# Token DFT in a spectral mixer: the fifth channel block accumulates T1, and a group has 28 steps in place of 32

## The chip, the cores and the metric

The kernel runs on one core of a Trainium2 chip, as one program. The core has a matrix engine (PE, which writes its results into eight banks called PSUM), a vector engine (DVE), a scalar engine (ACT), GpSimd (POOL) and SyncE (SP); the last two mostly issue DMA transfers here. Every engine takes its instructions in the order of the program and waits for semaphores of the others. The metric is the time of one execution in microseconds, the median of several runs.

## What is computed

The input `x` has 2048 tokens of 640 channels. The output is the sum of `x`, a two-dimensional Fourier transform of the normalized input (real part), and an MLP over the tokens:

```python
xn = _layernorm(x)
a = einsum("bsd,ed->bse", xn, dft_hid_re);  b = einsum("bsd,ed->bse", xn, dft_hid_im)
y = einsum("ts,bse->bte", dft_seq_re, a) - einsum("ts,bse->bte", dft_seq_im, b)
...
u = gelu(einsum("bsd,sf->bdf", _layernorm(xn), w1) + b1)
out = x + y + transpose(einsum("bdf,fs->bds", u, w2) + b2)
```

All values are float32.

## The kernel before

**Stages.** The kernel does the transform over tokens first (the "column" stage), stores its real and imaginary halves in DRAM (`y_part`), then does the transform over channels (`hidden`), then the two halves of the MLP (`up`, `down`). Only the column stage is touched.

**Float32 by three matmuls.** A float32 operand is cut in two: `high` copies it into a rounded format (ACT), and `low` subtracts the rounded copy from the original (DVE). `three` then multiplies high by high, high by low and low by high, all into one bank. Of the two operands of a column product, the channels of `x` stand in SBUF already cut (`fixed`), and the matrix is cut piece by piece: `cut_piece` makes a piece of 128 by 512 with one `high` (line 138) and one `low` (line 141). Three buffers take the pieces in turn.

**A group.** `columns` makes one group of the column stage: 512 output tokens `c`, for one half `h` of the input tokens. There are seven groups (a first block of columns is made by `first_columns`); the first three of them have `h` = 0 and store with plain writes, the last four have `h` = 1 and add to what stands in DRAM (`store_y`, lines 455 and 457, both from POOL's queue). In a group, four matrix blocks B11, B21 (real) and B12, B22 (imaginary), each of four pieces q = 0 to 3, meet five blocks of 128 channels. The first four channel blocks are done as a two by two block product with seven products in place of eight (Winograd's form of Strassen's scheme), for which the blocks of the matrix are replaced in place by T1 = B12 - B11, T3 = B22 - B12, T2 = B22 - T1 and T4 = B21 - T2. Products 1, 2, 5, 6, 3, 7 and 4 take B11, B21, T1, T2, B22, T3 and T4. Each takes six matmuls for a piece: three for each of two halves e = 0, 1 of 128 channels.

**The fifth channel block** takes part in no such scheme: it needs the plain sums F0 = A1 B11 + A2 B21 and F1 = A1 B12 + A2 B22, where A1 and A2 are its upper and lower rows of tokens. Its three matmuls ride on the pieces of product 1 (B11), 2 (B21) and 3 (B22). No product of the scheme takes B12 plain, so B12 is cut as a piece of its own ("product 8"), with no other matmuls than those three. A group thus has 32 pieces or steps, with 9, 3 or 6 matmuls each, 216 in all.

**What sets the order.** A hand-written turn (`turn_of`) emits for step i, on every engine: the loads due, the reads of banks, the `high` of step i + 2, the differences of matrix blocks (`extras`), a few jobs that prepare later stages (`do_jobs`, at the turns listed in `JOBS_AT`, in turns modulo `GROUP`), the `low` of step i + 2, and then the matmuls of step i. All offsets in `columns` count turns from the group's first step.

**Reading the banks.** Sums leave a bank in two ways: `fresh` copies a bank to one of the `c` tiles on ACT (line 601), and `more` adds a bank to the `c` tile on DVE (line 612) and stores it. There are six `c` tiles, which are handed out in turn by `c_tile`; a tile that comes round again is written only after the store that last read it has landed. C11, C12, C22 and C21 each have two halves e; F0 and F1 have one bank each (`psum[4]` and `psum[7]`). In the last group (`g == 2 * NC - 2`) C22 and C12 are not summed on DVE: each of their two parts is copied and stored by itself.

Of the kernel before, what the change touches and what calls it, by code (L numbers as in the profile page):

```python
# [17 lines left out]
F = 1728  # L18
# [8 lines left out]
NC = S // CH  # L27
# [23 lines left out]
    M6 A6 H4 T6 N4 B6 L4 b11 P5 H5 M7 A7 R6-7 T7 N5 B7 F6-7 L5 b12 e1 P6  # L51
    H6 T8 M8 A8 N6 B8 L6 b13 P7 H7 T9 M12 A12 N7 B9 L7
"""
GROUP = 32

JOBS_AT = (
    ((0, 1, 2, 3, 4, 5, 10, 20, 21, 26, 27, 30, 31), (0, 1, 2, 3, 20), ()),
    ((0, 1, 2, 3, 20, 21, 27, 31), (), (9, 11, 25)),  # L60
)


# [6 lines left out]
def fnet_plus_mixer(  # L70
# [30 lines left out]
    nc = tc.nc  # L101
# [41 lines left out]
    def sub(to, a, b):  # L143
        nc.vector.tensor_sub(to, a, b)  # L144

    def three(psum, w, m, first, last):

        (wh, wl), (mh, ml) = w, m
        nc.tensor.matmul(psum, wh, mh, start=first, stop=False, skip_group_check=True)  # L149
        nc.tensor.matmul(psum, wh, ml, start=False, stop=last and wl is None, skip_group_check=True)  # L150
        if wl is not None:
            nc.tensor.matmul(psum, wl, mh, start=False, stop=last, skip_group_check=True)  # L152
# [17 lines left out]
    def cut_piece(source, n, tail=False, stacked=False):  # L170

        held = {}

        def of_tail():
            hi, src = (t.rearrange("p (q c) -> p q c", c=P) for t in (held["piece"][:, 0, :n], source()))
            return hi[:, :, :TAIL], hi[:, :, P - TAIL :], src[:, :, :TAIL]

        def top():  # L180
            cut_turn[0] = (cut_turn[0] + 1) % (AHEAD + 1)
            held["piece"] = keep.tile([P, 2, D], R32, name="piece", tag=f"cut{cut_turn[0]}")
            if tail:
                hi, _, src = of_tail()
                high(hi, src)
            else:
                high(held["piece"][:, 0, :n], source())

        def bottom():
            if tail:  # L190
                hi, lo, src = of_tail()
                low(lo, src, hi)
                return held["piece"][:, 0, :n], None
            hi, lo = (held["piece"][:, i, :n] for i in range(2))
            if stacked:
                last = slice(n - P, n)
                low(hi[TAIL:, last], source()[TAIL:, last], hi[TAIL:, last])
            whole = n - P if stacked else n
            low(lo[:, :whole], source()[:, :whole], hi[:, :whole])
            return hi, lo  # L200

        return top, bottom
# [89 lines left out]
    def fifth(a, which, i):  # L292
        return a[:, which, 7 * Q + i * P : 7 * Q + (i + 1) * P]
# [154 lines left out]
    def c_tile():  # L448

        i = c_turn[0] = (c_turn[0] + 1) % 6  # L450
        return c_place[i // 3][:, i % 3, :]

    def store_y(h, m, c, j, t):
        if h == 0:
            nc.gpsimd.dma_start(y_part[m][c][:, j, :], t)
        else:
            nc.gpsimd.dma_start(y_part[m][c][:, j, :], t, accum_op=ALU.add)
# [76 lines left out]
    def columns(g, h, c):  # L534

        s0 = len(steps)
        raw = [pieces[(g + m) % 2] for m in range(2)]
        banks, cs = {}, {}

        def load(name, q):  # L540
            i, m = int(name[1]) - 1, int(name[2]) - 1
            nc.sync.dma_start(raw[m][:, i, q, :], dft_seq[m * NC + c, 8 * h + q + 4 * i])

        for name, at in (("B11", (-6, -5, -5, -4)), ("B21", (-3, -3, -2, -2)), ("B12", (-2, -1, 0, 0)), ("B22", (1, 2, 3, 4))):
            for q in range(4):
                loads[s0 + at[q]].append(lambda name=name, q=q: load(name, q))

        def b(name, q, n=1):
            t = raw[int(name[2]) - 1][:, int(name[1]) - 1]
            return t[:, q, :] if n == 1 else t[:, q : q + n, :]  # L550

        order = [(1, q) for q in range(4)] + [(i, q) for q in range(4) for i in (2, 8)]
        order += [(i, q) for i in (5, 6) for q in range(4)]
        order += [(3, 0), (3, 1)] + [(7, q) for q in range(4)] + [(3, 2), (3, 3)] + [(4, q) for q in range(4)]
        operand = {1: "B11", 2: "B21", 5: "B11", 6: "B11", 3: "B22", 7: "B12", 8: "B12", 4: "B21"}
        for names, at in (
            (("B11", "B12", "B11"), (6, 8)), (("B11", "B22", "B11"), (13, 15)), (("B12", "B22", "B12"), (17, 18)),
            (("B21", "B21", "B11"), (22, 24)),  # L560
        ):
            for e in range(2):
                extras[s0 + at[e]].append(lambda names=names, e=e: sub(*(b(n, 2 * e, 2) for n in names)))

        bank_of = {1: "z", 6: "z", 7: "z", 4: "z", 5: "y", 3: "y", 2: "w"}
        bank_at = {"z": 2 - 2 * (g % 2), "y": 2 * (g % 2), "w": 5}
        fifth_of = {1: (0, 0), 2: (0, 1), 8: (1, 0), 3: (1, 1)}

        def products(i, q):
            def run(w):
                a = fixed[h][q]
                if q == 0 and i in (1, 2, 5):
                    for e in range(2):
                        banks[bank_of[i], e] = psum[bank_at[bank_of[i]] + e]
                if i in fifth_of:
                    m, low_rows = fifth_of[i]
                    first = q == 0 and i in (1, 8)
                    if first:  # L580
                        banks["f", m] = psum[4 + 3 * m]
                    three(
                        banks["f", m], (fifth(a, 0, low_rows), fifth(a, 1, low_rows)), w,
                        first, q == 3 and i in (2, 3),
                    )
                if i in bank_of:
                    for e in range(2):
                        at = slot[i] * Q + e * P
                        three(
                            banks[bank_of[i], e], (a[:, 0, at : at + P], a[:, 1, at : at + P]), w,  # L590
                            q == 0 and i in (1, 2, 5), q == 3,
                        )
            return run

        for i, q in order:
            steps.append(cut_piece(lambda i=i, q=q: b(operand[i], q), CH) + (products(i, q),))

        def fresh(name, at, key, e, then=None):
            def run():
                cs[name, e] = c_tile()  # L600
                nc.scalar.activation(cs[name, e], banks[key, e], AF.Copy)
                if then:
                    store_y(h, *then, cs[name, e])
            reads[s0 + at].append(run)

        def more(name, at, key, e, then):
            if g == 2 * NC - 2 and name != "C11":

                return fresh(name, at, key, e, then)

            def run():
                nc.vector.tensor_add(cs[name, e], banks[key, e], cs[name, e])
                store_y(h, *then, cs[name, e])
            reads[s0 + at].append(run)

        for e in range(2):
            fresh("C11", 4, "z", e)
            more("C11", 11 + e, "w", e, (0, c, e))
            last = g == 2 * NC - 2
            fresh("C22", 16, "y", e, (1, c, 2 + e) if last else None)  # L620
            fresh("C12", 20, "z", e, (1, c, e) if last else None)
            more("C12", 28 + e, "y", e, (1, c, e))
            more("C22", 26 + e, "z", e, (1, c, 2 + e))
            fresh("C21", 32, "z", e, (0, c, 2 + e))
        fresh("F0", 13, "f", 0, (0, c, 4))
        fresh("F1", 30, "f", 1, (1, c, 4))


    moving = {}
# [370 lines left out]
    for g in range(2 * NC - 1):  # L1000
        columns(g, (g + 1) // NC, (g + 1) % NC)
    s_rows = BLOCK
    s_half = BLOCK + (NC - 1) * GROUP
    s_hid = len(steps)
# [73 lines left out]
    with tc.manual_schedule():  # L1078
        for word in START.split():
            start[word[0]](*map(int, word[1:].split("-")))  # L1080
        for i in range(8, len(steps) + 1):
            n_jobs, short = (1, i < BLOCK), False
            if BLOCK <= i < s_hid - 6:
                *n_jobs, light = [(i - BLOCK) % GROUP in at for at in JOBS_AT[i >= s_half]]
                if light:
# [47 lines left out]
```

## Time and profile before

| | |
|---|---|
| median of 3 runs | 876.68 us (876.0 to 876.92) |
| the profiled execution, its own time | 875.92 us |
| its span (first to last instruction) | 874.2 us |
| PE busy | 869.0 us, 4924 matmuls |
| DVE busy | 711.7 us |
| ACT busy | 530.2 us |
| seven column groups, by PE | 61.97 to 405.36 us |

The profile is of one execution. Its page gives busy time by engine, the span in 40 slices, the chain of work that ended last, and groups of instructions by line of the kernel. A row of a group reads: line, engine, operation, output and input tiles with shapes, count, then busy time, mean of one in ns, and the idle time of that engine just before them with what ended it. A window row gives for each engine its busy time in the stretch and in brackets how many instructions were in it.

### The profile page before, as it was taken

The page shows a single profiled execution, that of the slowest core. Times are in us where ns is not written, and L with a number is a line of the kernel's source. Part 1 is how long each engine was busy: PE and PEld are TensorE (multiplying, and loading weights), DVE is VectorE, ACT ScalarE, POOL GpSimd, SP SyncE. Part 2 cuts the span into 40 slices and gives each one's busy share as a digit, 9 for nine tenths or more (in the row PEclk, how much of TensorE's full clock was granted, in tenths as well). Part 3 has the DMA queues.
Part 4 walks back from the last instruction along what each step waited for, and adds up shares of the span by engine and source line. Part 5 has one row for each costly group of instructions (what it writes and reads, how often), then busy time and mean ns, then how long its engine had stood idle before and what let it go on. Part 6 is the DMA issues. An engine that isn't in the chain of part 4 may idle for free.

```text
span 874.2 us, 13999 instructions
## 1 busy us (share of the span) xinstructions
PE 869.0 (99%) x4924; PEld 793.1 (91%) x4924; DVE 711.7 (81%) x1217; ACT 530.2 (61%) x960; POOL 126.2 (14%) x170
## 2 busy tenths in 40 slices
PE   9999999999999999999999999999999999999998
PEld 6888888888888888889999999999999999999998
DVE  7878878795887978788887787998678978897887
ACT  5746576764556566557565556675577766555553
POOL 0110100101121111222010101000212221111211
PEclk9999999999999999999999999999999999999999
DMA  7771554619385556869666756454678797766786
GB/s 270 231 266 76 194 203 132 242 59 357 54 219 92 163 119 133 208 92 195 168 127 166 156 139 196 162 177 138 142 170 181 169 244 193 190 136 133 151 173 139
DMA packets 86087, 147.64 MB, mean 169 GB/s; under 512 B 8512, under 2 KB 35904, under 8 KB 85760
## 3 DMA queue, kind: packets, MB, share of 16 engines
q1 hardware_dynamic: 64928, 95.80, 34.0%
q0 software_dynamic: 20800, 50.70, 30.6%
q8 instruction: 38, 0.62, 0.3%
q14 instruction: 33, 0.27, 0.1%
q10 hardware_dynamic: 288, 0.25, 0.1%
HBM read 99.96 MB, written 52.00 MB: 174 GB/s over the span
## 4 chain that ended last, share of the span: by engine, by line
PE 94%; DVE 3%; ACT 1%; DMA 1%; issue 1%; DVEq 0%; ACTq 0%
PE psum L149 30%; PE psum L150 30%; PE psum L152 29%; PE psum L477 5%; DVE piece L141 1%; DMA pieces<-y 1%; DVE pieces L144 0%; DMA x<-in_x 0%; ACT piece L138 0%; ACT n L259 0%; ACT x L259 0%; DVE pair L144 0%; DVE st L210 0%; DVE pieces L785 0%; DVE shid L141 0%
## 5 line engine op out<-in xcount | busy, mean ns | idle before, releaser
L141 DVE TENSOR_TENSOR piece<-pieces,piece 128x512 fp32r<-128x512 f32 (+2 forms) x524 | 350.1, 671 | 125.8 <-ACT piece L138 119.1
L138 ACT ACTIVATE piece<-pieces 128x512 fp32r<-128x512 f32 (+3 forms) x508 | 318.1, 627 | 212.0 <-PE psum L152 143.5
L150 PE MATMUL psum<-piece,n 128*128 128x512 f32 x504 | 196.4, 390 | 0.0
L149 PE MATMUL psum<-piece,n 128*128 128x512 f32 x504 | 196.2, 389 | 0.0
L152 PE MATMUL psum<-piece,n 128*128 128x512 f32 x504 | 196.1, 389 | 0.0
L149 PE MATMUL psum<-sup,piece 128*128 128x320 f32 x392 | 121.2, 310 | 0.0
L149 PE MATMUL psum<-sdown,piece 128*128 128x320 f32 x392 | 121.0, 309 | 0.0
L150 PE MATMUL psum<-sup,piece 128*128 128x320 f32 x392 | 120.9, 309 | 0.0
L150 PE MATMUL psum<-sdown,piece 128*128 128x320 f32 x392 | 120.9, 309 | 0.0
L152 PE MATMUL psum<-sup,piece 128*128 128x320 f32 x376 | 116.6, 310 | 0.0
L152 PE MATMUL psum<-sdown,piece 128*128 128x320 f32 x376 | 116.2, 309 | 0.0
L144 DVE TENSOR_TENSOR pieces<-pieces 128x512 f32<-128x512 f32 (+3 forms) x142 | 112.7, 794 | 2.6
L150 PEld LDWEIGHTS psum<-piece,n 128*128 128x128 f32 x504 | 94.6, 188 | 21.0 <-DVE piece L141 1.5
L149 PEld LDWEIGHTS psum<-piece,n 128*128 128x128 f32 x504 | 94.6, 188 | 19.9
L152 PEld LDWEIGHTS psum<-piece,n 128*128 128x128 f32 x504 | 94.6, 188 | 19.3
L152 PE MATMUL psum<-shid,piece 128*128 128x320 f32 x280 | 86.6, 309 | 0.1
L150 PE MATMUL psum<-shid,piece 128*128 128x320 f32 x280 | 86.5, 309 | 0.0
L149 PE MATMUL psum<-shid,piece 128*128 128x320 f32 x280 | 86.5, 309 | 0.0
L854 ACT ACTIVATE pair<-psum 128x320 f32<-128x320 f32 x102 | 44.5, 436 | 54.6 <-PE psum L152 49.8
L149 PEld LDWEIGHTS psum<-sup,piece 128*128 128x128 f32 x392 | 73.6, 188 | 0.6 <-ACT pairs L854 0.3
L149 PEld LDWEIGHTS psum<-sdown,piece 128*128 128x128 f32 x392 | 73.6, 188 | 0.2 <-ACT pair L852 0.2
L150 PEld LDWEIGHTS psum<-sup,piece 128*128 128x128 f32 x392 | 73.6, 188 | 0.0
(106 smaller groups left out, 1115.8 us busy)
## 6 DMA issues: line engine op xcount, KB each, us to landing
pieces<-in_dft_seq SPq DMA_DIRECT2D x128, 256.0 KB, 5.4
pieces<-in_w SPq DMA_DIRECT2D x88, 256.0 KB, 3.7
y<-c POOLq DMA_DIRECT2D x84, 256.0 KB, 6.1
out<-pair POOLq DMA_DIRECT2D x38, 320.0 KB, 5.3
pieces<-y SPq DMA_DIRECT2D x32, 320.0 KB, 3.9
pieces<-in_w SPq DMA_DIRECT2D x32, 192.0 KB, 3.1
out<-in_x SPq DMA_DIRECT2D x16, 320.0 KB, 7.1
up<-pair POOLq DMA_DIRECT2D x8, 640.0 KB, 3.2
```

The source lines that it names most:

```text
L138: nc.scalar.activation(hi, src, AF.Copy)
L141: nc.vector.tensor_sub(lo, src, hi.bitcast(F32))
L144: nc.vector.tensor_sub(to, a, b)
L149: nc.tensor.matmul(psum, wh, mh, start=first, stop=False, skip_group_check=True)
L150: nc.tensor.matmul(psum, wh, ml, start=False, stop=last and wl is None, skip_group_check=True)
L152: nc.tensor.matmul(psum, wl, mh, start=False, stop=last, skip_group_check=True)
L477: nc.tensor.matmul(banks[m, j], channels(k, j)[rows], w[cols], start=n == 0 and k == begin, stop=n == 2 and k == end, skip_group_check=True,)
L854: nc.scalar.activation(c, b, AF.Copy)
```

## The change

`GROUP` becomes 28. Product 8 and its four cuts of B12 are gone. The matmuls of the fifth channel block ride on other pieces: upper rows on product 1 (B11) and on product 5 (T1), both into the bank `psum[4]`; lower rows on product 2 (B21) into `psum[7]`, and on product 3 (B22) into `psum[4]`. After product 1 the bank holds A1 B11, after product 5 A1 B11 + A1 T1 = A1 B12, after product 3 F1. So A1 B11 is copied out of the bank after product 1 (`fresh("F", 4, ...)`), and F0 is made by adding `psum[7]` to that copy on DVE at turn 13, which then is stored. The four differences of blocks, the reads and the job slots get new turns.

```diff
-GROUP = 32
+GROUP = 28
 JOBS_AT = (
-    ((0, 1, 2, 3, 4, 5, 10, 20, 21, 26, 27, 30, 31), (0, 1, 2, 3, 20), ()),
-    ((0, 1, 2, 3, 20, 21, 27, 31), (), (9, 11, 25)),
+    ((0, 1, 2, 3, 4, 12, 14, 15, 18, 19, 20, 21, 22, 23, 26, 27), (0, 1, 2, 3), ()),
+    ((0, 1, 2, 3, 4, 19, 22, 27), (), (10, 14, 21)),
 )
...
-        order = [(1, q) for q in range(4)] + [(i, q) for q in range(4) for i in (2, 8)]
-        order += [(i, q) for i in (5, 6) for q in range(4)]
+        order = [(i, q) for i in (1, 2, 5, 6) for q in range(4)]
         order += [(3, 0), (3, 1)] + [(7, q) for q in range(4)] + [(3, 2), (3, 3)] + [(4, q) for q in range(4)]
...
-            (("B11", "B12", "B11"), (6, 8)), (("B11", "B22", "B11"), (13, 15)), (("B12", "B22", "B12"), (17, 18)),
-            (("B21", "B21", "B11"), (22, 24)),
+            (("B11", "B12", "B11"), (5, 7)), (("B12", "B22", "B12"), (6, 8)), (("B11", "B22", "B11"), (9, 11)),
+            (("B21", "B21", "B11"), (16, 17)),
...
-        fifth_of = {1: (0, 0), 2: (0, 1), 8: (1, 0), 3: (1, 1)}
+        fifth_of = {1: (0, 0), 2: (1, 1), 5: (0, 0), 3: (0, 1)}
...
-                    first = q == 0 and i in (1, 8)
+                    first = q == 0 and i in (1, 2)
...
-                        first, q == 3 and i in (2, 3),
+                        first, q == 3,
...
-            if g == 2 * NC - 2 and name != "C11":
+            if g == 2 * NC - 2 and name in ("C12", "C22"):
                 return fresh(name, at, key, e, then)
             def run():
-                nc.vector.tensor_add(cs[name, e], banks[key, e], cs[name, e])
-                store_y(h, *then, cs[name, e])
+                c = cs[name, 0 if name == "F" else e]
+                nc.vector.tensor_add(c, banks[key, e], c)
+                store_y(h, *then, c)
...
+        fresh("F", 4, "f", 0)
         for e in range(2):
-            fresh("C11", 4, "z", e)
-            more("C11", 11 + e, "w", e, (0, c, e))
+            fresh("C11", 4 + e, "z", e)
+            more("C11", 10 + 2 * e, "w", e, (0, c, e))
             last = g == 2 * NC - 2
-            fresh("C22", 16, "y", e, (1, c, 2 + e) if last else None)
-            fresh("C12", 20, "z", e, (1, c, e) if last else None)
-            more("C12", 28 + e, "y", e, (1, c, e))
-            more("C22", 26 + e, "z", e, (1, c, 2 + e))
-            fresh("C21", 32, "z", e, (0, c, 2 + e))
-        fresh("F0", 13, "f", 0, (0, c, 4))
-        fresh("F1", 30, "f", 1, (1, c, 4))
+            fresh("C22", 12, "y", e, (1, c, 2 + e) if last else None)
+            fresh("C12", 16, "z", e, (1, c, e) if last else None)
+            more("C12", 24 + e, "y", e, (1, c, e))
+            more("C22", 22 + e, "z", e, (1, c, 2 + e))
+            fresh("C21", 28, "z", e, (0, c, 2 + e))
+        more("F", 13, "f", 1, (0, c, 4))
+        fresh("F", 26, "f", 0, (1, c, 4))
```

More of the change, by code (lines that the diff above doesn't have):

```diff
@@ L550, in b @@
             return t[:, q, :] if n == 1 else t[:, q : q + n, :]
-        order = [(1, q) for q in range(4)] + [(i, q) for q in range(4) for i in (2, 8)]
-        order += [(i, q) for i in (5, 6) for q in range(4)]
+        order = [(i, q) for i in (1, 2, 5, 6) for q in range(4)]
         order += [(3, 0), (3, 1)] + [(7, q) for q in range(4)] + [(3, 2), (3, 3)] + [(4, q) for q in range(4)]
-        operand = {1: "B11", 2: "B21", 5: "B11", 6: "B11", 3: "B22", 7: "B12", 8: "B12", 4: "B21"}
+        operand = {1: "B11", 2: "B21", 5: "B11", 6: "B11", 3: "B22", 7: "B12", 4: "B21"}
         for names, at in (
-            (("B11", "B12", "B11"), (6, 8)), (("B11", "B22", "B11"), (13, 15)), (("B12", "B22", "B12"), (17, 18)),
-            (("B21", "B21", "B11"), (22, 24)),
+            (("B11", "B12", "B11"), (5, 7)), (("B12", "B22", "B12"), (6, 8)), (("B11", "B22", "B11"), (9, 11)),
+            (("B21", "B21", "B11"), (16, 17)),
         ):
```

## The prediction

> **What bounds the kernel now.** First the busy times of the page:
>
> ```profile
> span 874.2 us, 13999 instructions
> PE 869.0 (99%) x4924; PEld 793.1 (91%) x4924; DVE 711.7 (81%) x1217; ACT 530.2 (61%) x960; POOL 126.2 (14%) x170
> ```
>
> PE is busy for all but 5.2 us. A busy PE need not be a PE at its pace, so the waits of PE's matmuls come next; all that the view lists is two waits, both before the column groups:
>
> ```profile
> PE psum L135 <- DVE idle L132: 1.2, 1, 1.2
> PE psum L477 <- DVE piece L141: 0.2, 1, 0.2
> ```
>
> Last the windows of busy time (PE, PEld, DVE, ACT, POOL, clock, DMA). By count of matmuls the fifth group is exactly the first stretch; the next two lie in it and in the sixth; the last is of a later stage, with 320 columns a matmul:
>
> ```profile
> 258.26:307.29 49.03, 49.03 (x217) 40.46 (x216) 39.39 (x55) 28.98 (x49) 8.60 (x10) 1.00 0.62 142
> 287.00:297.00 10.00, 10.00 (x45) 8.13 (x45) 9.60 (x14) 5.90 (x10) 0.00 (x0) 1.00 0.31 86
> 307.00:317.00 10.00, 10.00 (x45) 8.29 (x45) 6.96 (x12) 7.62 (x14) 1.73 (x2) 1.00 1.01 229
> 430.00:500.00 70.00, 70.00 (x480) 70.00 (x479) 55.64 (x81) 37.56 (x62) 8.55 (x10) 1.00 0.71 162
> ```
>
> A group has 216 matmuls (the 217th in brackets is a neighbour's): 49.03 / 216 = 0.227 us from one to the next. That pace holds whether DVE is busy for 9.60 of 10 us or for 6.96: 45 matmuls both times. The granted clock is 1.00 in all. So the groups are bound by the count of matmuls, and cutting is hidden. I write times in a group from its start: n matmuls take 0.227 n.
>
> **The change part by part.**
>
> *Matmuls.* The fifth block has three matmuls on 16 pieces before (products 1, 2, 8, 3) and after (1, 2, 5, 3). The sum is 12 x 9 + 4 x 6 + 2 x 9 + 4 x 6 + 2 x 9 + 4 x 6 = 216 again: 49.03 us, change 0.
>
> *Cuts removed, adds added.* Four pieces in each of seven groups:
>
> ```profile
> L141 DVE TENSOR_TENSOR piece<-pieces,piece 128x512 fp32r<-128x512 f32 x33 | 22.7, 690 | 9.3 <-ACT piece L138 9.0
> ```
>
> ```profile
> L138 ACT ACTIVATE piece<-pieces 128x512 fp32r<-128x512 f32 x32 | 20.2, 631 | 19.1 <-PE psum L152 15.1 <-DVE piece L141 2.2 <-DVE pieces L144 1.1
> L601 ACT ACTIVATE c<-psum 128x512 f32<-128x512 f32 x10 | 5.9, 595 | 1.0 <-PE psum L152 0.6
> ```
>
> ACT loses 28 x 0.631 = 17.7 us, DVE 28 x 0.690 = 19.3 us and gains seven adds of about 0.69 (row below), 4.8 us. All of it lies under PE, which never waits there: worth 0.
>
> *The new wait.* Six `c` tiles go round. In the new order the seventh taken in a group, for the second half of C12 (turn 16), is the first again, F's, whose store is issued only at turn 13. ACT must wait for that store to land, and behind it on ACT stands the `high` of step 18. Before, F0's tile came round again only at turn 32. The working goes by rows of the fifth group. Up to product 5 there are 108 matmuls and up to product 6 132, before as after, so the copies of C22 and C12 keep their times; rows of ACT, then DVE, then POOL:
>
> ```profile
> 282.26 1.28 ACT L601 ACTIVATE c<-psum 128x512 f32<-128x512 f32 x2
> 283.43 0.62 ACT L138 ACTIVATE piece<-pieces 128x512 fp32r<-128x512 f32 x1
> ...
> 287.70 1.28 ACT L601 ACTIVATE c<-psum 128x512 f32<-128x512 f32 x2
> ```
>
> ```profile
> 276.14 0.69 DVE L612 TENSOR_TENSOR c<-psum,c 128x512 f32<-128x512 f32 x1
> ...
> 284.09 0.69 DVE L141 TENSOR_TENSOR piece<-pieces,piece 128x512 fp32r<-128x512 f32 x1 [0.37 <-ACT piece L138]
> 284.70 1.22 DVE L144 TENSOR_TENSOR pieces<-pieces 128x1024 f32<-128x1024 f32 x1
> 285.83 0.69 DVE L141 TENSOR_TENSOR piece<-pieces,piece 128x512 fp32r<-128x512 f32 x1
> ```
>
> ```profile
> 277.12 0.85 POOL L457 DMA_DIRECT2D y<-c  x1 [16.72 <-DVE c L612]
> ```
>
> The C22 copies (24.00) are followed by a `high` (25.17) and its `low` (284.09, that is 25.83); the next DVE work starts at 284.70, 26.44. After the change that next work is F's add: 26.44 + 0.69 = 27.13. POOL issues 0.29 after an add ends (276.14 + 0.69 to 277.12): F's store is issued at 27.42. The next `low`, of step 15, then ends by 26.44 + 0.61 + 0.69 = 27.74; PE wants it in the second matmul of step 15, at (126 + 1) x 0.227 = 28.83, so the add itself delays nothing.
>
> Two copies take 1.28 and one 0.60 (the group of ten above), so the second starts 0.68 after the first: for C12 at 287.70 + 0.68, that is 30.12, if nothing holds it. Let it start at x. `high` of step 18 starts 0.49 later (as 283.43 after 282.94) and ends at x + 1.11; its `low` ends at x + 1.84; then T4's second half (turn 17) and the `low` of step 19 behind it, x + 1.15 + 0.61 + 1.13 + 0.69 = x + 3.58. PE wants the first of these at (150 + 1) x 0.227 = 34.28, the second at 157 x 0.227 = 35.64. So x may be 32.06, and beyond that PE loses what x loses. How long a store takes, for a plain write and for adds in DRAM (pairs of stores; the second lands later):
>
> ```profile
> L455 POOL DMA_DIRECT2D y<-c x3: 539/539/539, 179.7 to 181.6; - x3
> ...
> DMA to landing us min/median/max: 2.3/2.3/2.6
> ```
>
> ```profile
> L457 POOL DMA_DIRECT2D y<-c x2: 850/1022/1193, 279.1 to 279.6; - x2
> ...
> DMA to landing us min/median/max: 4.4/5.2/6.0
> ```
>
> ```profile
> L457 POOL DMA_DIRECT2D y<-c x2: 847/948/1050, 381.2 to 381.9; - x2
> ...
> DMA to landing us min/median/max: 4.1/4.6/5.1
> ```
>
> ```profile
> L457 POOL DMA_DIRECT2D y<-c x2: 847/1020/1193, 377.1 to 377.7; - x2
> ...
> DMA to landing us min/median/max: 5.3/5.7/6.1
> ```
>
> And how soon an engine starts after a landing (412.53 + 5.25 = 417.78 to 417.88, 0.10), in the chain of waits:
>
> ```profile
> 412.53 5.25 DMA pieces<-y
> ...
> 417.88 0.84 DVE pieces L785
> ```
>
> Groups 1 to 3 write plainly: F lands at 27.42 + 2.6 = 30.0 at the latest, before ACT asks (30.12). Change 0.
>
> Groups 4 to 6 add in DRAM. C11's second add stands behind the `low` of step 13, whose `high` may start when step 10 has ended (99 x 0.227 + 0.2 = 22.7), so it ends at about 24.6 and its store goes out at 24.9, some 2.5 us before F's; F's is then like the first of a pair: 4.1 to 4.4. x = 27.42 + 4.4 + 0.1 = 31.9 at most: ACT idles 1.5 to 1.8 us, PE does not. I take 0; bounds 0 and, at the 6.0 of a store close behind another, 33.52 - 32.06 = 1.5 a group.
>
> In group 7 C22 is stored at once, twice, at turn 12 around C11's second store; so F's is the fourth within 2.5 us. The first is issued at 24.00 + 0.60 + 0.29 = 24.9 and lands 4.1 later, at 29.0. A store behind another lands after it by 381.9 + 5.1 - 381.2 - 4.1 = 1.7, by 2.1 (279) or by 1.4 (377). Three of them at 1.7: F lands at 34.1, x = 34.2, PE loses 34.2 - 32.06 = 2.1 us. Bounds with 1.4 and 2.1: 1.2 and 3.3. Nothing later makes it up, as PE is full to the end.
>
> *Differences and jobs moved.* Turns 5 to 9 carry a `low` (0.61 to the next start) and a difference (1.13), 1.74 us in a step of 9 x 0.227 = 2.04. T3 now needs B22 at turn 6, on DVE at about 11.7 (the `low` of step 7 may start after step 4 has ended, 10.2, plus a `high`). The loads before it, issue and landing:
>
> ```profile
> L542 SPq DMA_DIRECT2D pieces<-in_dft_seq x6: 327/402/424, 299.5 to 304.8; - x6
> ...
> DMA to landing us min/median/max: 6.7/9.8/11.0
> ```
>
> The last lands at 304.8 + 11.0 = 315.8, 8.5 into the next group: 3.2 to spare, and only if that were gone would DVE stand before T3 with all cuts behind it. The loads keep their places on SP's queue. The early copy of F's bank is done by about 9, product 5 writes there at 72 x 0.227 = 16.3. The jobs are the same ones at other turns; of a group's 49.03 us DVE was busy for 39.39, and now has four `low` less and one add more, 37.3. All these I take at 0; together I allow up to 0.5 us for a turn in which they crowd.
>
> *Sum.* 0 + 0 + 2.1 + 0.1 of the small ones = 2.2. The span of 874.2 becomes 876.4, the execution's own 875.92 becomes 878.1. (The 1.7 us around the span stay.) The median shown is 0.76 above that execution: **878.9 us**, 0.25% more.
>
> The Trainium skill, page "DMA: Bandwidth & Descriptors", section "Anatomy of one DMA — SWDGE (gpsimd) path", gives such a transfer 2.0 us plus its bytes at 436 a ns, by estimate 2.6 us for 256 KB; the plain writes agree (2.3 to 2.6), the adds do not (4.1 to 6.1). By that rule F would land at 30.0 in all groups, nothing would wait, and the outcome would be the first rival's.
>
> **The rivals.**
>
> *Not slower: the last group's stores overlap.* If the four stores run side by side and F's lands within 4.5 us of its issue (x up to 32.06), no group stalls. For it: a lone add lands in 4.1. Against it: the pairs land 1.4 to 2.1 apart. Time: 876.68 plus at most 0.5 of the small ones, say 876.7.
>
> *All four late groups stall.* If F's store takes 6.0 in groups 4 to 6 too, each loses 1.5: 2.2 + 4.4, 883.3 us. For it: 6.0 was seen in the same quiet stretch of a group. Against: only for a store issued 0.5 us behind another.
>
> *Faster: PE's pace depends on the others.* From 0.227 at 512 columns and 70 / 480 = 0.146 at 320, a matmul has a part of 0.011 us that does not go with columns. If DVE and ACT caused it and it shrank with the cuts, by 28 of 224, 1512 matmuls would gain 1512 x 0.011 / 8 = 2.1 us: 874.6. Against it: the equal windows above.
>
> [...]
>
> **How the numbers follow.** Forecast 0.58, no stall 0.25, all four 0.14, faster 0.03. About 0.2% (1.75 us) is what a measurement of this kernel can tell from no change. The forecast's bounds (1.2 to 3.8 with the small ones) put some four fifths of it over 1.75: slower 0.46 + 0.14 = 0.60; within 0.2%: 0.12 + 0.25 = 0.37; faster 0.03. The likeliest case's own range is 877.9 to 880.5; the whole one reaches from the no-stall case to the four stalls, 876.2 to 883.3.
>
> **What would show it.** In the new profile: 4924 matmuls; ACT's cuts shorter by 17.7 us; waits of ACT's `c` on the DMA of `y<-c` four times, 1.5 to 1.8 us three times and about 4 us once; no such wait in groups 1 to 3; six groups of 49.0 us and a seventh of about 51.2, with a gap on PE at steps 18 and 19 of it alone. Equal groups of 49.0 would mean the stores overlap; gaps of 1.5 us in groups 4 to 6, the second rival; a gap at turns 5 to 9, that B22 or the moved differences come late; a pace below 0.227 us, the third. I am wrong in kind if PE waits anywhere for something other than the piece behind C12's copy.

## The result and the profile after

| | before | after |
|---|---|---|
| median of 21 runs each | 876.29 us (875.54 to 876.92) | 877.66 us (877.1 to 879.56) |
| the profiled execution, its own time | 875.92 us | 877.1 us |
| its span | 874.2 us | 875.3 us |

The ratio on record for these runs is 1.0021, with a 95% interval of 1.0014 to 1.0027: slower. The two medians are 1.37 us apart, which is a ratio of 1.0016. The predicted time was 878.9 us. The execution profiled after the change is the fastest of its 21.

The busy times of the page of the kernel after, and from its groups of instructions the row of the cuts of `pieces` by `high`, then the same row of the kernel before:

```profile
span 875.3 us, 13921 instructions
PE 868.4 (99%) x4924; PEld 793.4 (91%) x4924; DVE 698.5 (80%) x1196; ACT 511.3 (58%) x932; POOL 126.2 (14%) x170
...
L138 ACT ACTIVATE piece<-pieces 128x512 fp32r<-128x512 f32 (+2 forms) x480 | 299.8, 627 | 219.2 <-PE psum L152 152.1
```

```profile
L138 ACT ACTIVATE piece<-pieces 128x512 fp32r<-128x512 f32 (+3 forms) x508 | 318.1, 627 | 212.0 <-PE psum L152 143.5
```

The 4924 matmuls are all there. ACT has 28 instructions fewer and is busy for 18.9 us less, DVE has 21 fewer and is busy for 13.2 us less. So 32 us of work is gone from the two engines, and the span is 1.1 us longer. PE sets the time, so its waits come next, then those of ACT's copies into `c` (engine, line, what is waited for, and then the total, the number of waits and the longest):

```profile
PE psum L135 <- DVE idle L132: 1.2, 1, 1.2
PE psum L477 <- DVE norm L235: 0.9, 1, 0.9
PE psum L149 <- ACT piece L138: 0.7, 1, 0.7
PE psum L150 <- DVE piece L141: 0.2, 1, 0.2
PE psum L477 <- DVE piece L141: 0.2, 1, 0.2
...
ACT c L600 <- DMA y<-c: 8.8, 5, 3.7
```

Lines 149 and 150 are matmuls of `three`: PE now waits twice for a piece inside the column groups, and ACT five times for a store. The wait of 0.9 us for `norm` is new too, but stands ahead of the groups and costs nothing: by PE's timelines the matmul behind it starts at 6.50 us, and in the kernel before it starts at 6.51. Only the idle matmuls ahead of it end sooner here. The windows of the fifth, sixth and seventh group say where (each from the first matmul of the group to the first of what follows):

```profile
257.78:306.74 48.96, 48.96 (x218) 40.54 (x216) 37.80 (x54) 25.84 (x45) 8.58 (x10) 1.00 0.61 137
306.74:355.70 48.96, 48.96 (x218) 40.54 (x216) 38.97 (x55) 27.36 (x48) 8.57 (x10) 1.00 0.61 140
355.70:406.55 50.85, 49.84 (x217) 40.38 (x216) 37.80 (x60) 27.78 (x50) 12.04 (x14) 1.00 0.72 136
```

By the starts of PE's matmuls the seven groups take 48.99, five times 48.96, and 50.85 us; before they took 49.05, 49.18 and five times 49.03. The seventh loses 50.85 - 48.96 = 1.89 us. The sum went from 343.39 to 344.64.

The seventh group from its start at 355.70, in the timeline of ACT (start, duration, line, operation; in brackets the idle time before it and its releaser):

```profile
385.14 0.60 ACT L600 ACTIVATE c<-psum 128x512 f32<-128x512 f32 x1
...
389.41 0.60 ACT L600 ACTIVATE c<-psum 128x512 f32<-128x512 f32 x1 [3.68 <-DMA y<-c]
```

Behind the copy stands the `high` of step 18, and on PE, in the timeline of matmuls, the first and the second matmul of step 18:

```profile
390.58 0.49 PE L149 MATMUL psum<-piece,n 128*128 128x512 f32 x1 [0.72 <-ACT piece L138]
391.30 0.50 PE L150 MATMUL psum<-piece,n 128*128 128x512 f32 x1 [0.23 <-DVE piece L141]
```

The first half of C12 is copied at once and the second waits 3.68 us for its tile, until 389.41, which is 33.71 of the group. The first matmul of step 18 then has to wait for its `high`, the second for its `low`. The five matmuls with a gap, three of step 18 and two of step 19, are late by 0.88, 0.50, 0.11, 0.23 and 0.11 us, together the 1.83 of the 1.89 that stands in gaps over 0.015 us.

What F's store did, by the view of POOL's stores in two stretches of the seventh group (first all four of turns 11 to 13; then F's and the one ahead of it, of which F's took the 6.2 us): the spread of the issues, the wait that they ended, and the time from issue to landing:

```profile
L457 POOL DMA_DIRECT2D y<-c x4: 847/1080/1529, 380.6 to 383.1; - x4
...
  ACT c L600: 3.7, 1
...
DMA to landing us min/median/max: 4.2/5.9/6.4
...
DMA to landing us min/median/max: 6.2/6.3/6.4
```

F's goes out at 383.12, 27.42 of the group, as the fourth within 2.53 us, and lands at 389.31, after 6.19 us; 0.10 later ACT copies. The four land at 384.76, 386.72, 388.04 and 389.31.

The same place in the fifth group (start 257.78), first in POOL's timeline, then in the view of that store, then in ACT's timeline:

```profile
285.19 0.85 POOL L457 DMA_DIRECT2D y<-c  x1 [1.62 <-DVE c L612]
```

```profile
L457 POOL DMA_DIRECT2D y<-c x1: 855/855/855, 285.2 to 285.2; - x1
...
DMA to landing us min/median/max: 4.1/4.1/4.1
```

```profile
289.36 0.60 ACT L600 ACTIVATE c<-psum 128x512 f32<-128x512 f32 x1 [1.54 <-DMA y<-c]
```

F's store goes out at 27.41 here, 2.46 us behind the store ahead of it, lands 4.1 us later, and ACT copies at 31.58 after 1.54 us of idling. PE is on time: the group takes 48.96 us.

### The profile page after: what moved, and what is told of

Read it like the earlier page. It is cut to its first block, busy times and chain, and to the rows that moved or that the text cites. A ratio compares the mean times of both kernels' runs of the same rounds, so it can differ in the third digit from the quotient of the medians.

```text
span 875.3 us, 13921 instructions
## 1 busy us (share of the span) xinstructions
PE 868.4 (99%) x4924; PEld 793.4 (91%) x4924; DVE 698.5 (80%) x1196; ACT 511.3 (58%) x932; POOL 126.2 (14%) x170
## 4 chain that ended last, share of the span: by engine, by line
PE 55%; DVE 0%; DVEq 0%; issue 0%
PE psum L149 18%; PE psum L150 18%; PE psum L152 18%; DVE piece L141 0%; DVE pieces L144 0%; DVE pair L847 0%; DVEq L1130 0%
## 5 line engine op out<-in xcount | busy, mean ns | idle before, releaser
L141 DVE TENSOR_TENSOR piece<-pieces,piece 128x512 fp32r<-128x512 f32 (+4 forms) x496 | 330.8, 669 | 141.4 <-ACT piece L138 138.0
L138 ACT ACTIVATE piece<-pieces 128x512 fp32r<-128x512 f32 (+2 forms) x480 | 299.8, 627 | 219.2 <-PE psum L152 152.1
L149 PEld LDWEIGHTS psum<-sup,piece 128*128 128x128 f32 x392 | 73.6, 188 | 0.6 <-ACT pairs L855 0.3
L149 PEld LDWEIGHTS psum<-sdown,piece 128*128 128x128 f32 x392 | 73.6, 188 | 0.4 <-ACT pair L853 0.2
L150 PEld LDWEIGHTS psum<-sdown,piece 128*128 128x128 f32 x392 | 73.6, 188 | 0.0
```

The costliest lines, as they stand in the source:

```text
L138: nc.scalar.activation(hi, src, AF.Copy)
L141: nc.vector.tensor_sub(lo, src, hi.bitcast(F32))
```

## The experiments

The theory: the only loss is the wait of C12's second copy for F's `c` tile, and it reaches PE in the last group alone, because four stores that add in DRAM stand within 2.5 us there and land one after the other. The rivals: something else about the last group or the new turns costs the time (the late add of F itself, the differences, the jobs); or the four removed cuts a group matter, in one direction or the other. Each kernel is the kernel after with the edit shown, but for the last.

### Another tile for C12's second half

```diff
-        fresh("F", 4, "f", 0)
+        fresh("F", 6, "f", 0)
```

F's copy is taken after both of C11's, so the tile that comes round at turn 16 is C11's first one.

> The changed kernel with F's copy out of its bank at turn 6 in place of 4, so that the six c tiles come round in another order: the second half of C12 now takes the tile of C11's first half, stored at turn 10, and nobody takes F's tile before turn 28. F's add and store, all stores and POOL's queue stay. Theory (what costs time is the wait for F's tile): F's store in group 7 still lands about 33.6 us after the group's start, no copy on ACT waits for a store, all seven groups take 48.96 us on PE, and the time is 1.9 us below the changed kernel's 877.66, about 875.8, some 0.5 below the kernel before (ratio 0.9994). Rival (group 7 is late because its four stores or the order of DVE's work around T4 hold up the cuts): the gap of 1.8 us at steps 18 and 19 of group 7 stays and the time is 877.7.

The median was 875.38 us, before in the same series 875.88: ratio 0.9994 (0.9986 to 1.0003). The window of the seventh group, and the landing of the store ahead of F's and of F's own:

```profile
355.84:404.80 48.96, 48.96 (x218) 40.54 (x216) 37.99 (x60) 27.95 (x50) 12.07 (x14) 1.00 0.73 137
```

```profile
L457 POOL DMA_DIRECT2D y<-c x2: 968/1248/1529, 381.8 to 383.3; - x2
...
DMA to landing us min/median/max: 6.3/6.4/6.5
```

F's store still took 6.3 us, nothing waited for it, and the group took 48.96. The stores are as slow as before; only who waits for the tile has changed. Against before, the median of this kernel is 0.50 us lower where that of the changed one is 1.37 higher. The difference of 1.87 agrees with the 1.89 of the seventh group, although each of the two is known only to some 0.7 us.

### F's store two turns later

```diff
-        more("F", 13, "f", 1, (0, c, 4))
+        more("F", 15, "f", 1, (0, c, 4))
```

> The changed kernel with F's add and store at turn 15 in place of 13; the tiles come round as in it. F's store is then issued about 2.2 us later, near 29.65 of a group. Theory (PE loses what C12's second copy starts after 31.8 to 32.1): in groups 1 to 3 plain writes land by about 32.0 to 32.2, 0 to 0.4 us lost each; in groups 4 to 6 the adds land at 33.7, 1.7 to 2.0 lost each; in group 7 the queue of stores has drained, 1.9 to 2.3 lost as before. Sum: 5 to 7 us above the changed kernel, 882.7 to 884.7. Rival (only the pile of four stores in group 7 can hold PE): at most 0.4 us more than 877.66.

The median was 884.46 us: ratio 1.0096 (1.008 to 1.0111). Windows of the third, the fifth and the seventh group:

```profile
160.37:209.60 49.23, 49.23 (x218) 40.48 (x216) 36.22 (x55) 26.67 (x48) 5.41 (x10) 1.00 0.47 172
260.65:311.57 50.92, 49.87 (x218) 40.38 (x217) 37.85 (x54) 25.72 (x45) 8.59 (x10) 1.00 0.57 128
362.50:413.91 51.41, 49.85 (x218) 40.39 (x217) 37.91 (x60) 27.79 (x50) 12.07 (x14) 1.00 0.72 135
```

The store went out at 29.65 in place of 27.42. The plain writes of groups 1 to 3 landed 2.3 us later, ACT copied at 32.04 to 32.11, and PE lost 0.2 to 0.3 us; the adds of groups 4 to 6 landed 4.0 to 4.1 later, ACT copied at 33.74 to 33.87, and PE lost some 2.0. All seven groups now fit one rule: PE loses what the copy's start exceeds about 31.8 by (32.04 - 0.25; 33.8 - 2.0; in the kernel after 33.71 - 1.89 = 31.82). The prediction had this limit at 32.06.

### The last group's C22 stores behind F's

```diff
-            fresh("C22", 12, "y", e, (1, c, 2 + e) if last else None)
+            fresh("C22", 12, "y", e)
+            if last:
+                reads[s0 + 14].append(lambda e=e: store_y(h, 1, c, 2 + e, cs["C22", e]))
```

> The changed kernel; only in group 7 the two early stores of C22 are issued at turn 14 in place of 12, so that they stand behind F's store on POOL's queue. The tiles come round as in the changed kernel. Theory (F's store is late there only because it is the fourth in a row): it is issued at 27.4 and lands near 31.5 as in groups 4 to 6, ACT waits 1.5 us in four groups, PE loses nothing, and the time is 1.8 us below 877.66, about 875.9. Rival (the wait for a tile costs in every late group, or group 7 is slow for another reason): the time stays at 877.5 or above.

The median was 875.41 us: ratio 0.9993 (0.9984 to 1.0002). The wait for the tile, and the seventh group:

```profile
ACT c L600 <- DMA y<-c: 7.2, 5, 1.7
```

```profile
355.66:404.62 48.96, 48.96 (x218) 40.54 (x216) 37.91 (x60) 27.89 (x50) 12.05 (x14) 1.00 0.75 140
```

The copy started at 31.69 in the seventh group, as in the groups before it, and PE lost nothing. So it is the two stores ahead of F's that make the difference of the last group.

### The last group's stores as plain writes

```diff
+        elif c == NC - 1:
+            nc.gpsimd.dma_start(y_part[m][c][:, j, :], t)
```

This stands ahead of the adding branch of `store_y`; the order of the stores is that of the kernel after. The last group's output then leaves out the part of the first half of the tokens.

> The changed kernel; the last 512 output columns of the second half of the tokens (group 7) are stored with plain writes in place of adds, so that the first half's part is left out of them. Theory (four adds in DRAM within 2.5 us queue up, 1.3 to 2.0 us each): plain writes go out 0.54 us apart and land 2.3 to 3.0 later, F by 30.4, so ACT hardly waits in group 7 and PE loses nothing there; 1.8 us below 877.66, about 875.8. Groups 4 to 6 still add and wait on ACT for 1.5 us. Rival (the fourth store is late because of POOL's queue, not of the adds): the loss in group 7 stays above 1 us.

The median was 874.96 us, before in the same series 875.89: ratio 0.9988 (0.9979 to 0.9998), some 0.8 us under the expectation. Half of that lies in the series, in which before ran 0.4 us lower than the 876.29 that goes with 877.66. The seventh group took 48.96 us, and the waits are:

```profile
ACT c L602 <- DMA y<-c: 5.6, 4, 1.6
```

The four stores of turns 11 to 13 landed 2.33 to 2.82 us after their issue here. Four stores in 2.5 us do not hold the tile if they are plain writes. It takes the queue and the adding together.

### The four cuts of a group made twice

```diff
-    def cut_piece(source, n, tail=False, stacked=False):
+    def cut_piece(source, n, tail=False, stacked=False, again=False):
+        turns = 2 if again else 1
...
-                high(held["piece"][:, 0, :n], source())
+                for _ in range(turns):
+                    high(held["piece"][:, 0, :n], source())
...
-            low(lo[:, :whole], source()[:, :whole], hi[:, :whole])
+            for _ in range(turns):
+                low(lo[:, :whole], source()[:, :whole], hi[:, :whole])
...
+            twice = (i, q) in ((2, 1), (2, 3), (5, 1), (5, 3))
-            steps.append(cut_piece(lambda i=i, q=q: b(operand[i], q), CH) + (products(i, q),))
+            steps.append(cut_piece(lambda i=i, q=q: b(operand[i], q), CH, again=twice) + (products(i, q),))
```

> The changed kernel with the work of 28 cuts put back: steps 5, 7, 9 and 11 of each group make their high and their low twice (the second time the same values). Theory (cuts are hidden under PE and worth nothing): ACT is busy for 17.7 us more, DVE for some 17 to 19 us more, PE's groups stay at 48.96 us (group 7 at 50.9), and the time is 877.7 within 0.5. Rival (PE's pace or its waits depend on how much ACT and DVE cut): groups get longer, by up to 0.3 us each, 2 us in all.

The median was 883.18 us: ratio 1.0083 (1.0069 to 1.0097). This expectation failed, though the work put back was as meant (ACT busy for 17.2 us more, DVE for 16.3). The wait for the tile, then the second and the fourth group:

```profile
ACT c L604 <- DMA y<-c: 12.2, 5, 4.3
```

```profile
110.76:162.03 51.27, 50.57 (x217) 40.08 (x216) 42.21 (x70) 33.23 (x61) 5.41 (x10) 1.00 0.48 172
...
212.60:261.56 48.96, 48.96 (x218) 40.55 (x216) 36.31 (x51) 26.78 (x46) 7.95 (x10) 1.00 0.63 185
```

The groups took 48.99, 51.27, 50.57, 48.96, 49.78, 49.48 and 51.52. The fourth bears the cuts for nothing. The second and third lose 2.3 and 1.6 us, 1.6 in each of them at steps 6 to 12. The rest came through the tile. In the second group F's plain write took 4.59 us, and PE lost 0.7 at steps 18 and 19. In the fifth and sixth group C11's store slid from 24.95 to 26.14 and 25.51, so that F's stood closer behind it and took 5.12 and 4.79 us in place of 4.1, the copy started at 32.64 and 32.31, and PE lost 0.82 and 0.52. (In the fifth group C11's own store took 5.09 us, so the smaller distance is not shown to be the only reason there.) Two causes are mixed here, so the next two kernels are to part them.

### The cuts made twice, with the other tile

The same edit together with `fresh("F", 6, "f", 0)`; in the second of the two kernels only groups 4 to 7 cut twice:

```diff
-            twice = (i, q) in ((2, 1), (2, 3), (5, 1), (5, 3))
+            twice = g >= 3 and (i, q) in ((2, 1), (2, 3), (5, 1), (5, 3))
```

> The work of 28 cuts put back as in e4_cuts_back, on top of e1_ring, so that no copy waits for F's tile. e4_cuts_back lost 1.47 us in each of groups 2 and 3 at the matmuls of steps 5 to 11, and 0.5 to 2.6 us in groups 2, 5, 6 and 7 at those of steps 18 and 19. Theory (two separate causes: DVE has no room for the cuts in groups 2 and 3, where two jobs a turn run in turns 0 to 3; and later stores of C11 push F's store back, whose tile is waited for): the second part goes, the first stays: e1_ring's 875.38 plus 2.9, 878.3. Rival (one cause: all of it comes by the tile): 875.4. Other rival (all of it is DVE): 882 or more.

> As e8_cuts_ring, but the cuts are made twice only in groups 4 to 7 (16 cuts put back). Theory (a cut is hidden wherever no two jobs stand in a turn): 875.4 within 0.5, all seven groups 48.96 to 49.05 us. Rival (each cut costs PE something): in proportion to e8_cuts_ring's, 16 of 28 of what it loses, 1.7 us, 877.1.

With all groups cut twice the median was 877.42 us, ratio 1.0017 (1.0008 to 1.0027); with groups 4 to 7 it was 875.08, ratio 0.9991 (0.9981 to 1.0). Windows of the first kernel's second and fourth group:

```profile
110.88:160.96 50.08, 49.74 (x218) 40.24 (x217) 42.39 (x70) 33.02 (x61) 5.39 (x10) 1.00 0.51 186
...
211.02:259.98 48.96, 48.96 (x218) 40.55 (x217) 36.35 (x51) 27.11 (x46) 7.93 (x10) 1.00 0.63 186
```

and DVE's timeline in its second group, where that stretch's matmul with the longest wait follows in PE's timeline:

```profile
122.00 0.42 DVE L144 TENSOR_TENSOR later<-later 128x256 f32<-128x256 f32 x1
122.67 0.69 DVE L141 TENSOR_TENSOR piece<-pieces,piece 128x512 fp32r<-128x512 f32 x1 [0.25 <-ACT piece L138]
123.28 1.22 DVE L144 TENSOR_TENSOR pieces<-pieces,pieces 128x1024 f32<-128x1024 f32 x1
124.64 1.42 DVE L141 TENSOR_TENSOR piece<-pieces,piece 128x512 fp32r<-128x512 f32 x2
```

```profile
126.12 0.50 PE L150 MATMUL psum<-piece,n 128*128 128x512 f32 x1 [0.34 <-DVE piece L141]
```

Groups 2 and 3 take 50.07 and 50.06, all others 48.96 but for the first, 49.01. Each loses 1.1 us: jobs for later stages (`later`), a difference of blocks and the cuts made twice stand on DVE in a row, and PE waits for the `low` at their end. In the second kernel all groups from the second on take 48.96, the four with four pieces cut twice among them. So four more cuts a group cost nothing in groups 4 to 7, as the prediction had it for the four removed ones, and 1.1 us in groups 2 and 3 of the new schedule. That is not what the removed cuts cost before: there groups 2 and 3 held them and took 49.18 and 49.03. Nor is it the amount of work: in the first 18.4 us of the group DVE is busy for 15.2 in group 1, which loses nothing, and for 13.9 in groups 2 and 3. What in their order of work makes the difference was not tested.

The first expectation was right in kind and 0.9 us too high. The other tile takes 0.5 us off each of the two groups as well: with F's copy at turn 4 ACT makes two copies in a row ahead of the `high` of step 6, which starts 11.61 us into the second group, and with the copy at turn 6 it starts at 11.13. The two causes are not quite apart.

### The late store with the other tile

Both `fresh("F", 6, "f", 0)` and `more("F", 15, "f", 1, (0, c, 4))`.

> Both edits at once: F's add and store at turn 15 as in e3_f_late, and F's copy at turn 6 as in e1_ring, so that no copy takes F's tile before turn 28. Theory (the late store costs only through the wait for its tile): F lands as late as in e3_f_late (33.7 in groups 4 to 6), nobody waits for it, and the 9 us between e3_f_late (884.46) and e1_ring (875.38) are gone: 875.4 within 0.5. Rival (the late add itself, on DVE between the cuts, holds PE up): 880 or more.

The median was 875.14 us: ratio 0.9992 (0.9982 to 1.0001). The fifth group, which had lost 2.0 us with the late store alone:

```profile
257.85:306.81 48.96, 48.96 (x218) 40.54 (x216) 38.14 (x54) 26.06 (x45) 8.58 (x10) 1.00 0.60 139
```

No copy waited for a store. A late add and a late store cost only through the tile.

### Before, with one difference a turn later

The groups of the kernel before take 49.03 and those after take 48.96, which the prediction had not foreseen. The suspect is a near miss: a piece that is ready a moment after PE could have used it, too little to show in the view of waits. In the kernel before, the second matmul of step 20 takes 0.41 us in place of 0.39 in groups 3 to 7, the third starts 0.024 late, and some nine behind it are late by less: 0.07 us together. DVE's and PE's timelines there, in the fifth group:

```profile
286.43 1.22 DVE L144 TENSOR_TENSOR pieces<-pieces 128x1024 f32<-128x1024 f32 x1
287.57 1.29 DVE L141 TENSOR_TENSOR piece<-pieces,piece 128x512 fp32r<-128x512 f32 x2
```

```profile
288.40 0.41 PE L150 MATMUL psum<-piece,n 128*128 128x512 f32 x1
288.65 0.40 PE L152 MATMUL psum<-piece,n 128*128 128x512 f32 x1
```

The first of the two `low` at 287.57 is that of step 20. It stands behind T3's second difference and ends just as PE wants it. The edit is to the kernel before:

```diff
-            (("B11", "B12", "B11"), (6, 8)), (("B11", "B22", "B11"), (13, 15)), (("B12", "B22", "B12"), (17, 18)),
+            (("B11", "B12", "B11"), (6, 8)), (("B11", "B22", "B11"), (13, 15)), (("B12", "B22", "B12"), (17, 19)),
```

> The kernel before with one difference moved: the second half of T3 at turn 19 in place of 18, so that the low of step 20 no longer stands behind it on DVE. In the kernel before, groups 2 to 7 show 0.07 us more than the changed kernel's 48.96 (some ten matmuls from the 134th on, the second of step 20, come 5 to 25 ns late), and group 2 another 0.15 at steps 8 and 9. Theory (what the changed groups gain is only that near miss of the low of step 20): groups 3 to 7 take 48.96 us, group 2 about 49.1, and the time is 0.4 us below the kernel before, 875.5 (ratio 0.9995). Rival (PE's pace itself got better with less cutting on ACT and DVE): groups stay at 49.03 and the time at 875.9.

The median was 875.22 us, before in the same series 875.54: ratio 0.9998 (0.9989 to 1.0007), which tells no difference. The trace does. The groups took 48.99, 49.17 and five times 48.96; the second had been expected at about 49.1 and kept its loss at step 8. The fifth:

```profile
257.83:306.79 48.96, 48.96 (x217) 40.54 (x216) 39.40 (x55) 28.98 (x49) 8.60 (x10) 1.00 0.60 141
```

DVE and ACT are as busy as in the kernel before (39.39 and 28.98), with all cuts of B12 in place, and the group takes 48.96. So the 0.07 us in each of groups 3 to 7 was that one near miss, and no slower pace under more cuts.

## Why the prediction was right, and where it was off

**Matmuls, worth 0.** Right: 4924 matmuls, 216 a group, and in groups without a wait 48.96 / 216 = 0.2267 us from one to the next.

**Cuts removed, worth 0.** The busy times fell about as said (ACT by 18.9 us for 17.7, DVE by 13.2 for 19.3 - 4.8 = 14.5). The step that failed is "PE never waits there". The view of waits showed none, but the matmuls of step 20 came late, by 0.07 us together in five groups and 0.03 in the first two, and in the second group some 0.18 us more was lost at step 8. The groups without a stall gained 0.64 us in all (343.39 less 344.64 - 1.89): this is the term of the sum that was missing. Some 0.44 of it came from the place of a difference, as the last experiment shows, whose groups took 342.95. The other 0.2, of the second group, stays open: the change moved cuts, differences and jobs there at once, and no run parts them. The windows chosen for the argument lay in the fifth and sixth group; the ones without room are the second and third, where four more cuts cost 1.1 us each.

**The new wait.** F's store was forecast to be issued at 27.42 of a group and was, in groups 2 to 7; it was 27.44 in the first. That C12's second copy waits for it, and that the `high` of step 18 queued behind it carries the wait to PE, was shown by taking another tile, which removed it.

**Groups 1 to 3, no wait.** Missed in the second group: there F's plain write took 4.2 us, where 2.6 was the most allowed for, and the copy waited 0.5. That it cost PE nothing was luck: the start at 31.71 was 0.1 us under the limit. In the kernel with C22's stores behind F's and in the one with plain writes the same copy started at 31.92 and 31.98, and PE lost 0.11 and 0.17 us in the second group, which gives the limit of 31.8 again.

**Groups 4 to 6, ACT idles 1.5 to 1.8 us and PE does not.** Right: landings after 4.00, 4.06 and 4.11 us for the 4.1 to 4.4 assumed, waits of about 1.5. The copy started at 31.52 to 31.63, 0.2 to 0.3 us ahead of a limit that was 31.8 and not 32.06. The second rival (all four late groups stall) did not come about, but with C11's stores pushed back by the doubled cuts a stall of its kind appeared in two groups, of 0.82 and 0.52 us.

**Group 7.** The mechanism was right, the size a little high: F's store landed at 33.61, not 34.1, since the stores behind the first landed 1.96, 1.32 and 1.27 apart and not 1.7 each. The earlier limit gave half of that back: 33.71 - 31.82 = 1.89 us lost for the 2.1 forecast. By the timelines of DVE and PE most of the 0.24 between the limits is of three parts: PE wants the `low` of step 19 at 157 x 0.2267 = 35.59 and not 35.64, its matmul starts 0.05 behind that `low`, and the next matmul follows 0.34 later in place of 0.23.

**Small things, 0.1.** A loss was allowed for turns that crowd; none was seen. No gap stands at turns 5 to 9, nor does B22 come late.

**Sum.** The prediction had 2.1 + 0.1 = 2.2 us on the execution profiled; the groups gave 1.89 - 0.64 = 1.25, and the span 1.1. The forecast also added 0.76 us from the execution profiled to the median, taken from three runs; over 21 runs the kernel after has 0.56. So the direction and its cause were right, and the size was not: 877.66 lies 0.2 us under the range given for the likeliest case, 877.9 to 880.5. The first rival (all stores overlap) falls with the landings; so does the third, a pace that depends on the other engines, since 48.96 us holds with DVE busy for 36.3 or for 39.4 us.

The kernels that keep the change without its wait (another tile, or the stores in another order) run at 0.9992 to 0.9994 of before with intervals that hold 1. The change without its wait is not told apart from no change in the measured times. The traces leave it some 0.6 us, most of it of the near misses.

## What to carry to other kernels

When buffers go round in a ring and a change takes one fewer or frees one later, follow each tile to its next writer, and ask what stands behind that writer on its engine: here the copy into an innocent tile held up the cut that the bound engine needed. A store's time is not one number; count the stores that are issued just ahead of it on the same queue, and read the group in which most of them meet. A list of waits that is empty does not mean there is no slack to lose or gain; compare the lengths of equal groups to hundredths, and make the argument for every group whose order of work differs, not for a typical one. The busy share of an engine did not tell which group had room.

## What the runs showed of the hardware

**Adds in DRAM queue where plain writes don't.** In the kernel after, a 256 KB store that adds in DRAM landed 4.0 to 4.1 us after its issue when none had gone out in the 2.4 us before it, and four in 2.5 us landed 1.3 to 2.0 us apart, the last after 6.19. A plain write took 2.3. With the last group's stores as plain writes, the same four took 2.33 to 2.82 and held up no matmul.

**One plain write took nearly twice the usual time.** In the kernel after, F's plain write in the second group took 4.2 us and the third group's 2.3. The views of these two stores:

```profile
L455 POOL DMA_DIRECT2D y<-c x1: 539/539/539, 138.3 to 138.3; - x1
...
  ACT c L600: 0.5, 1
...
DMA to landing us min/median/max: 4.2/4.2/4.2
```

```profile
L455 POOL DMA_DIRECT2D y<-c x1: 539/539/539, 187.3 to 187.3; - x1
...
DMA to landing us min/median/max: 2.3/2.3/2.3
```

The view of DMA queues in the stretch of the first of them (packets, MB, share of the 16 engines' time) has a line that is missing in the other's:

```profile
q0 software_dynamic: 80, 0.26, 15.9%
...
q8 instruction: 1, 0.02, 2.1%
```

A packet of the instruction queue moved while that store was under way. The same holds in six of the experiments, where the second group's store took 4.2 to 4.6 us. In the two kernels with F's store two turns later it went out 0.6 and 1.0 us after that packet had begun to move, and took 2.3. This is a coincidence in nine kernels and was not tested by itself. An add did not always suffer: F's of the fifth group of the kernel after had such a packet beside it and took 4.06 us.
